# Grouped-query attention on one core: K of two pairs in one buffer, on alternating partitions

## The chip, the cores and the metric

The kernel runs on one core of one Trainium2 chip. The metric is the time of one execution on the device, in microseconds (us). A core has five engines with programs of their own, which meet at semaphores: TensorE (PE), VectorE (DVE), ScalarE (ACT), GpSimd (POOL) and SyncE (SP). Sixteen DMA engines move data between HBM and the on-chip memory SBUF, which has 128 partitions. SP issues nearly all loads here, in the order of its program.

## The reference

```python
B, Hq, Hkv, Sq, Sk, D = 16, 32, 8, 16, 2048, 128      # bf16
k = jnp.repeat(k, 4, axis=1)                           # four query heads share a key head
v = jnp.repeat(v, 4, axis=1)
scores = jnp.einsum("bhqd,bhkd->bhqk", q, k) * D ** -0.5
p = softmax(scores, axis=-1)
return jnp.einsum("bhqk,bhkd->bhqd", p, v)
```

There are 16 x 8 = 128 key heads. Each has 2048 keys and values of 128 numbers (512 KB of K, 512 KB of V) and 4 x 16 = 64 query rows. K and V are 134 MB together, and each byte of them is read once.

## The kernel before

The unit of work is a pair p of neighbouring key heads, 0 to 63: 1 MB of K, 1 MB of V and 128 query rows. Per pair:

- SP loads K into one of eight buffers `Kn` (128 partitions of 8 KB) and V into one of four buffers `Vb`. The helper `load` (L178, issuing through L173) describes a transfer by 64 rows of 16 KB in HBM and 128 rows of 8 KB in SBUF; the first two K loads are plain ones (L285) with 8 KB on both sides.
- DVE turns K with one 32x32-block transpose over 2048 columns of 4 bytes, each holding two bf16 numbers, into one of two buffers `KT` (`kt`, L482; it signals `sem_kt`).
- PE multiplies queries and keys, 32 matmuls into PSUM (`scores`, L353); there is one score buffer `S_ps`, so scores of the next pair wait for `sem_max`.
- DVE evicts and scales the scores in two halves and takes the smallest value of each row (L502; signals `sem_max`). POOL exchanges the row values between the halves of a pair (`exchange`, L225 to L240).
- ACT takes the exponential (L550), PE transposes the result P in eight pieces (L371), ACT evicts them to `PT` (L561), PE multiplies with V (`product`, L423; from pair 56 on in another arrangement, L412), and ACT divides by the row sum (`norm`, L574) and stores.

PE works on `scores(p+1)`, `product(p-4)` and `transposes(p)` in step p. DVE in step p evicts the scores of p, then turns K of p+2.

SP's order of loads is written out by a loop:

```python
for t in range(NP + VLAG):          # NP = 64, VLAG = 6
    if t < NP:
        load_k(t)
    ...                             # Q of four pairs, now and then
    if 0 <= t - VLAG < NP:
        load_v(t - VLAG)
```

SP waits in this order, so a wait holds everything behind it. K of pair p waits until K of pair p-8 has been turned; V of pair p waits until the product of pair p-4 has ended. V of the last four pairs goes into K buffers that are free by then, and waits for `sem_kt`. From pair 56 on (`P4`), V is loaded in two halves, with rows of 8 KB in HBM and 4 KB in SBUF, and the very last V in rows of 3 KB and 1 KB. Outputs go out through `NO` = 8 buffers from ACT's queue up to pair 39; later ones are held in SBUF and stored at the end. In the last steps PE's program is written out by hand, with idle matmuls between products (`IDLE`, L433).

Of the kernel before, what the change touches and what calls it, by code (L numbers as in the profile page):

```python
# [6 lines left out]
ALU = mybir.AluOpType  # L7
# [5 lines left out]
NV = 4  # L13
NKT = 2
NPT = 4
NO = 8
NQ = 2
NR = 8
VLAG = 6
PVLAG = 4  # L20
QLEAD = 3
HELD = (4, 4, 4, 4, 4, 3)
# [3 lines left out]
def bass_standalone__gqa_softmax__sampling_kernel(  # L26
# [3 lines left out]
    v: bass.AP,  # L30
    out: bass.AP,
):

# [21 lines left out]
    sb = lambda name, shape, dt: ctx.enter_context(nc.sbuf_tensor(name, shape, dt))  # L55
    sem = lambda name: ctx.enter_context(nc.semaphore(name))

    iota_t = sb("iota_t", [128, 128], I32)
    ident4 = sb("ident4", [128, 128], F32)
    warm = sb("warm", [128, 2], F32)  # L60
    Kn = [sb(f"Kn{i}", [128, 32 * 128], BF16) for i in range(NK)]
    Vb = [sb(f"Vb{i}", [128, 32 * 128], BF16) for i in range(NV)]
    KT = [sb(f"KT{i}", [128, 32 * 64], F32) for i in range(NKT)]
    Qn = [sb(f"Qn{i}", [128, 4, 128], BF16) for i in range(NQ)]
    Q4 = sb("Q4", [128, 4, 2, 4, 64], BF16)
    QT = [sb(f"QT{i}", [128, 2, 512], F32) for i in range(2)]
# [15 lines left out]
    O_ps = ctx.enter_context(nc.psum_tensor("O_ps", [128, 512], F32))  # L82

    sem_id = sem("sem_id")
    sem_k = [sem(f"sem_k{i}") for i in range(NK)]
    sem_v = [sem(f"sem_v{i}") for i in range(NV)]
    sem_vl = [sem(f"sem_vl{i}") for i in range(2)]
    sem_vx = [sem(f"sem_vx{i}") for i in range(3)]
# [20 lines left out]

    qf = q.rearrange("b h s d -> (b h s) d")  # L110
    of = out.rearrange("b h s d -> (b h s) d")
    kf = k.rearrange("b h s d -> (b h s d)").rearrange("(r x) -> r x", x=4096)
    vf = v.rearrange("b h s d -> (b h s d)").rearrange("(r x) -> r x", x=4096)
    vf4 = v.rearrange("b h s d -> (b h) (s d)").rearrange("g (a x) -> a g x", a=128)

# [15 lines left out]


    def v_tile(p):
        return Kn[p % 4 + (NP - 8) % NK] if p >= NP - 4 else Vb[p % NV]

    def out_tile(p, i):
        return Oh[:, p - PH, :] if isinstance(p, int) and PH <= p < NP - 1 else Osb[i % NO][:, :]
# [48 lines left out]
    with nc.Block() as block:  # L186

        @block.gpsimd
        def _(gp):
            gp.memset(warm[:, :], 0.0).then_inc(sem_id, 1)  # L190
            gp.iota(iota_t[:, :], [[1, 128]], base=0, channel_multiplier=-1).then_inc(sem_id, 1)
            gp.wait_ge(sem_id, 2)
            gp.tensor_scalar(ident4[:, :], iota_t[:, :], 0.0, None, op0=ALU.is_equal).then_inc(sem_id, 1)


            def held(p):
# [79 lines left out]

        @block.sync
        def _(sp):
            def load_k(p):
                s = p % NK  # L280
                if p >= NK:
                    sp.wait_ge(sem_kt, p - NK + 1)
                src = kf[128 * p:128 * (p + 1), :]
                if p < 2:
                    ins = sp.dma_start(Kn[s][:, :], src)  # L285
                else:
                    ins = load(sp, Kn[s][:, :], src, 4096, 2)
                ins.then_inc(sem_k[s], 16)

            def load_v(p):  # L290
                if p >= NP - 4:
                    sp.wait_ge(sem_kt, p - 3)
                elif p >= NV:
                    sp.wait_ge(sem_pv, p - NV + 1)
                dst = v_tile(p)[:, :]
# [12 lines left out]

            def store_held(p, n):
                sp.wait_ge(sem_nm, p + n + 1)  # L310
                src = Oh[:, p - PH:p - PH + n, :]
                copy(
                    sp, of[128 * p:128 * p + 128, :], [[128, 128], [128 * 128, n], [1, 128]],
                    src, [src.ap[0], [1, 1], [1, n * 128]],
                ).then_inc(sem_oh, 16)

            for t in range(NP + VLAG):
                if t < NP:
                    load_k(t)
# [12 lines left out]

        @block.tensor
        def _(pe):
# [3 lines left out]

            def scores(p, i, first=False):
                pe.wait_ge(sem_qs, p + 1)  # L340
                pe.wait_ge(sem_kt, p + 1)
                if not first:
                    pe.wait_ge(sem_max, p)
                kt = KT[i % NKT][:, :].bitcast(BF16).rearrange(
                    "p (w x b l f) -> p w b f x l", w=2, x=16, b=2, l=32)
                qs = Qs[i % 2][:, :, :].rearrange("p b (x f) -> p b f x", f=2)
                for acc in range(4):
                    b, f = divmod(acc, 2)
                    for r in range(4):
                        rows = slice(32 * r, 32 * (r + 1))  # L350
                        h = r // 2
                        for w in range(2):
                            ins = pe.matmul(  # L353
                                S_ps[64 * w:64 * (w + 1), 512 * r:512 * (r + 1)],
                                qs[rows, b, f, 64 * h:64 * (h + 1)],
                                kt[rows, w, b, f],
                                start=(acc == 0), stop=(acc == 3),
                            )
                ins.then_inc(sem_s, 1)
# [29 lines left out]
            def product(p, i, out, tail=False, last=False):  # L389
# [13 lines left out]
                pe.nop(nofuse=True)  # L403
                if isinstance(p, int) and p >= P4:
                    pt = PT[i % NPT][:, :, :].bitcast(BF16).rearrange("p (h t) (w q e) -> p h w t e q", h=2, w=2, e=2)
                    vt = v_tile(p)[:, :].rearrange("p (h j d) -> p h j d", h=2, d=128)
                    for j in range(16):
                        w, t, e = j // 8, j % 8 // 2, j % 2
                        if last and j in (0, 12):
# [5 lines left out]
                            )  # L415
                else:
                    pt = PT[i % NPT][:, :, :].bitcast(BF16).rearrange("p t (w q e) -> p w t e q", w=2, e=2)
                    vt = v_tile(p if isinstance(p, int) else i)[:, :].rearrange("p (x d) -> p x d", d=128)
# [52 lines left out]

        @block.vector
        def _(dve):
            def kt(p, i):
                src = Kn[i % NK][:, :].bitcast(F32)
                dst = KT[i % NKT][:, :]
                if isinstance(p, int) and p >= P4:

                    src = src.rearrange("p (m x y) -> p m x y", m=2, x=8)
                    dst = dst.rearrange("p (x m y) -> p m x y", m=2, x=8)  # L480
                dve.wait_ge(sem_k[i % NK], 2 * (p - i) + 16 * (i // NK + 1))
                ins = dve.transpose(dst, src)  # L482
                ins.then_inc(sem_kt, 1)

# [5 lines left out]
            def step(p, i):  # L490
                known = isinstance(p, int)
                dve.wait_ge(sem_s, p + 1)
                if i >= 2:
                    dve.wait_ge(sem_exp, p - 1)
                for h in range(2):
                    if not known or p < P4:
                        dst = Sneg[i % 2][:, :].rearrange("p (t h g l e) -> p h g t l e", t=8, h=2, g=2, e=2)[:, h]
                        src = S_ps[:, 1024 * h:1024 * (h + 1)].rearrange("p (g t e l) -> p g t l e", g=2, t=8, e=2)
                    else:
                        dst = Sneg[i % 2][:, :].rearrange("p (h t g l f) -> p h g t l f", h=2, t=4, g=2, f=4)[:, h]  # L500
                        src = S_ps[:, 1024 * h:1024 * (h + 1)].rearrange("p (g t f l) -> p g t l f", g=2, t=4, f=4)
                    ins = dve.tensor_scalar(  # L502
                        dst, src,
                        -scale, None, op0=ALU.mult, op1=ALU.min, accum_out=own[:, i % NR, h:h + 1],
                    )
                ins.then_inc(sem_max, 1)
                if i >= 3 and i % 2:
                    recip(p - 3, i - 3, 2)
                if not known or p + 2 < NP:
                    kt(p + 2, i + 2)  # L510

            dve.wait_ge(sem_q[0], 16)
            spread(dve, 0, 1).then_inc(sem_q4d, 2)
# [7 lines left out]
        def _(act):  # L521
# [44 lines left out]
            def norm(p, i):  # L566
# [1 line left out]
                act.wait_ge(sem_pv, p + 1)  # L568
                act.wait_ge(sem_rec, p + 1)
                if not isinstance(p, int) or p < PH:  # L570
                    act.wait_ge(sem_o[i % NO], 2 * (p - i) + 16 * (i // NO + 1))
                elif p == NP - 1:
                    act.wait_ge(sem_o[i % NO], 16 * (PH // NO + 1))
                act.activation(  # L574
# [66 lines left out]
```

## Time and profile before

| | |
|---|---|
| median of 3 runs | 334.89 us (334.74 to 334.95) |
| profiled execution | 334.85 us, its span 333.5 us |
| busy: PE, DVE, ACT, POOL | 279.2, 294.5, 257.7, 149.4 us |
| DMA | 138.61 MB in 19583 packets, 416 GB/s in the mean |
| K loads | 64, of 1 MB, 20.2 us from issue to landing |
| V loads of 1 MB | 56, 18.2 us from issue to landing |
| transposes of K on DVE | 64, 2308 ns each |
| evictions of scores on DVE | 128 halves, 1206 ns each |

Times in a view count from the start of the span. Busy is the time in which an engine ran instructions. A line of the timeline gives start, duration, engine, line of the kernel, operation, and what was written from what; brackets give the idle time ahead of it and what ended it. A view of waits names the waiting engine and line, what ended the wait, the total in us, how often, and the longest. The chain of waits gives start, duration and what; SPq is SP's queue.

### The profile page before, as it was taken

The page shows a single profiled execution, that of the slowest core. Times are in us where ns is not written, and L with a number is a line of the kernel's source. Part 1 is how long each engine was busy: PE and PEld are TensorE (multiplying, and loading weights), DVE is VectorE, ACT ScalarE, POOL GpSimd, SP SyncE. Part 2 cuts the span into 40 slices and gives each one's busy share as a digit, 9 for nine tenths or more (in the row PEclk, how much of TensorE's full clock was granted, in tenths as well). Part 3 has the DMA queues.
Part 4 walks back from the last instruction along what each step waited for, and adds up shares of the span by engine and source line. Part 5 has one row for each costly group of instructions (what it writes and reads, how often), then busy time and mean ns, then how long its engine had stood idle before and what let it go on. Part 6 is the DMA issues. An engine that isn't in the chain of part 4 may idle for free.

```text
span 333.5 us, 16075 instructions
## 1 busy us (share of the span) xinstructions
PE 279.2 (84%) x6542; PEld 209.4 (63%) x6542; DVE 294.5 (88%) x354; ACT 257.7 (77%) x482; POOL 149.4 (45%) x488
## 2 busy tenths in 40 slices
PE   2585988999998999888897988979879798788877
PEld 1253756767676776666665766757757567666465
DVE  3999988999999999989898898998999999989940
ACT  3277877989898989779688787887788687776873
POOL 4444554364544555354445435354363453542320
DMA  8999999999999999999999999999999999999998
GB/s 314 426 419 422 413 419 415 431 424 422 426 423 425 420 428 420 430 418 426 422 427 420 431 419 425 424 423 425 419 421 424 415 423 421 417 425 414 412 405 293
DMA packets 19583, 138.61 MB, mean 416 GB/s; under 512 B 8432, under 2 KB 9712, under 8 KB 10864
## 3 DMA queue, kind: packets, MB, share of 16 engines
q1 hardware_dynamic: 13520, 136.95, 98.1%
q10 hardware_dynamic: 6048, 1.48, 2.0%
q8 instruction: 8, 0.13, 0.2%
q14 instruction: 7, 0.06, 0.0%
HBM read 136.31 MB, written 2.10 MB: 415 GB/s over the span
## 4 chain that ended last, share of the span: by engine, by line
DMA 57%; PE 16%; DVE 15%; issue 8%; ACT 1%; SPq 1%; POOL 1%; DVEq 0%; POOLq 0%; ACTq 0%
DMA Vb<-in_v_dram 43%; PE O_ps L423 9%; DMA Kn<-in_k_dram 8%; DVE KT L482 8%; DVE Sneg L502 7%; DMA Kn<-in_v_dram 5%; PE ST_ps L371 3%; PE S_ps L353 3%; ACT P L550 1%; SPq L173 1%; PE ST_ps L386 1%; POOL nbias L233 0%; PE ST_ps L412 0%; POOL oth L225 0%; POOL oth L228 0%
## 5 line engine op out<-in xcount | busy, mean ns | idle before, releaser
L482 DVE STREAM_TRANSPOSE KT<-Kn 128x2048 f32<-128x2048 f32 x64 | 147.7, 2308 | 20.1 <-DMA Kn<-in_k_dram 19.9
L550 ACT ACTIVATE P<-Sneg,nbias 128x1024 bf16<-128x1024 f32 x128 | 145.9, 1142 | 15.7 <-POOL nbias L233 14.2
L502 DVE TENSOR_SCALAR_CACHE_REDUCE Sneg<-S_ps 128x1024 f32<-128x1024 f32 x128 | 149.9, 1206 | 4.2 <-PE S_ps L353 4.2
L423 PE MATMUL O_ps<-Vb,PT 64*64 64x128 bf16 x3584 | 111.1, 216 | 30.5 <-issue 27.0
L423 PEld LDWEIGHTS O_ps<-Vb,PT 64*64 64x64 bf16 x3584 | 102.8, 107 | 49.3 <-issue 49.3
L561 ACT ACTIVATE PT<-ST_ps 128x512 f32<-128x512 f32 x126 | 68.5, 594 | 16.5 <-PE ST_ps L371 15.9
L353 PE MATMUL S_ps<-KT,Qs 32*64 32x512 bf16 x2048 | 73.5, 396 | 6.0 <-DVE Sneg L502 3.8
L371 PE MATMUL ST_ps<-ident,P 128*128 128x128 f32 x504 | 70.1, 283 | 8.7 <-ACT P L550 8.5
L225 POOL COPY oth<-own 64x4 f32<-64x4 f32 (+1 forms) x65 | 11.9, 183 | 136.4 <-DVE Sneg L502 134.3
L371 PEld LDWEIGHTS ST_ps<-ident,P 128*128 128x128 f32 x504 | 55.1, 143 | 16.9 <-ACT P L550 10.5
L353 PEld LDWEIGHTS S_ps<-KT,Qs 32*64 32x64 bf16 x2048 | 27.3, 106 | 30.4 <-issue 16.6
L207 POOL COPY Qs<-QT 128x512 bf16<-128x512 bf16 x64 | 39.0, 610 | 12.1 <-POOL rowsum L240 5.6
L233 POOL TENSOR_SCALAR nbias<-own,oth 128x1 f32<-128x1 f32 x128 | 33.9, 280 | 10.6 <-POOL oth L228 9.0
L163 POOL COPY Q<-Qn 128x1024 bf16<-128x1024 bf16 x31 | 32.4, 1044 | 1.4 <-DMA Qn<-in_q_dram 1.4
L574 ACT ACTIVATE O<-O_ps,rrec 128x128 bf16<-128x128 f32 x40 | 14.5, 363 | 18.7 <-PE O_ps L423 18.5
L240 POOL TENSOR_TENSOR rowsum<-own,oth 64x1 f32<-64x1 f32 x128 | 23.8, 186 | 8.2
L386 PE MATMUL ST_ps<-ident,Q 128*128 128x128 f32 x128 | 22.5, 304 | 4.6 <-POOL Q L163 4.6
L386 PEld LDWEIGHTS ST_ps<-ident,Q 128*128 128x128 f32 x128 | 14.7, 150 | 18.5 <-issue 18.5
L550 ACT ACTIVATION_READ_ACCUMULATOR P<-Sneg,nbias 128x1 f32 x128 | 24.2, 189 | 0.0
L536 ACT ACTIVATE QT<-ST_ps 128x512 f32<-128x512 f32 x32 | 18.5, 579 | 3.9 <-PE ST_ps L386 3.8
L574 ACT ACTIVATE Oh<-O_ps,rrec 128x128 bf16<-128x128 f32 x20 | 7.3, 367 | 17.3 <-PE O_ps L423 14.4
L228 POOL COPY oth<-own 64x4 f32<-64x4 f32 (+1 forms) x65 | 11.8, 181 | 7.3
(30 smaller groups left out, 44.6 us busy)
## 6 DMA issues: line engine op xcount, KB each, us to landing
Kn<-in_k_dram SPq DMA_DIRECT2D x64, 1024.0 KB, 20.2
Vb<-in_v_dram SPq DMA_DIRECT2D x56, 1024.0 KB, 18.2
Vb<-in_v_dram SPq DMA_DIRECT2D x8, 512.0 KB, 15.4
Kn<-in_v_dram SPq DMA_DIRECT2D x6, 512.0 KB, 14.5
Qn<-in_q_dram SPq DMA_DIRECT2D x15, 128.0 KB, 19.8
out_dram<-O ACTq DMA_DIRECT2D x41, 32.0 KB, 8.9
Kn<-in_v_dram SPq DMA_DIRECT2D x1, 768.0 KB, 17.7
out_dram<-Oh SPq DMA_DIRECT2D x5, 128.0 KB, 11.8
```

Of the source, the lines that this page charges most:

```text
L163: return eng.tensor_copy(Q4[:, :, b, :, :], src.unsqueeze(2).to_broadcast([128, 4, 4, 64]))
L207: gp.tensor_copy(Qs[i % 2][:, :, :], QT[i // 4 % 2][:, :, 128 * x:128 * (x + 1)].bitcast(BF16)).then_inc(sem_qs, 1)
L233: ins = gp.tensor_scalar(nbias[:, s, h:h + 1], own[:, s, h:h + 1], oth[:, s, h:h + 1], None, op0=ALU.min)
L240: gp.tensor_tensor(rowsum[rows, t:t + 1], own[rows, s, 2 + h:3 + h], oth[rows, s, 2 + h:3 + h], op=ALU.add,).then_inc(sem_sum[h], 1)
L353: ins = pe.matmul(S_ps[64 * w:64 * (w + 1), 512 * r:512 * (r + 1)], qs[rows, b, f, 64 * h:64 * (h + 1)], kt[rows, w, b, f], start=(acc == ...
L371: ins = pe.transpose(dst[:, 128 * t:128 * (t + 1)], P[i % 2][:, 128 * x:128 * (x + 1)], ident4[:, :])
L386: ins = pe.transpose(dst[:, 128 * j:128 * (j + 1)], src[:, j, b, :], ident4[:, :])
L423: ins = pe.matmul(out[rows, :], pt[rows, w, t, e, :], vt[rows, x, :], start=(x == 0), stop=(x == 31),)
L482: ins = dve.transpose(dst, src)
L502: ins = dve.tensor_scalar(dst, src, -scale, None, op0=ALU.mult, op1=ALU.min, accum_out=own[:, i % NR, h:h + 1],)
L550: ins = act.activation(to[:, h], of_s[:, h], ACT.Exp, bias=nbias[:, s, h:h + 1], scale=-1.0, accum_out=own[:, t, 2 + h:3 + h],)
L561: act.activation(PT[i % NPT][:, 4 * h:4 * (h + 1), :].rearrange("p t q -> p (t q)"), p_stage_ap(p, h), ACT.Copy,).then_inc(sem_ev[h], 1)
```

## The change

Two pairs, 2n and 2n+1, share a K buffer: there are four buffers `Kn` of 16 KB per partition instead of eight of 8 KB. Each pair lies on every other partition, the even pair on the even partitions, in rows of 16 KB, 64 keys to a row. So one transpose, over half of the columns of a buffer, turns half of the keys of both pairs, and two of them turn both pairs, into one of two buffers `KT` of twice the size. K of the first two pairs is loaded in four transfers of 8 KB rows, by halves of the keys.

With that, scores of an even pair wait for two transposes; the keys come in runs of 16 in `KT`, and the evictions put them in order. DVE turns K three steps ahead instead of two (two in step 0). V lags K by seven places in SP's loop instead of six. There are four output buffers instead of eight, and the table that the identity is made from lies in `KT[1]`.

```diff
-NO = 8
+NO = 4
-VLAG = 6
+VLAG = 7
...
-    Kn = [sb(f"Kn{i}", [128, 32 * 128], BF16) for i in range(NK)]
+    Kn = [sb(f"Kn{i}", [128, 64 * 128], BF16) for i in range(NK // 2)]
-    KT = [sb(f"KT{i}", [128, 32 * 64], F32) for i in range(NKT)]
+    KT = [sb(f"KT{i}", [128, 64 * 64], F32) for i in range(NKT)]
+    iota_t = KT[1][:, 0:128].bitcast(I32)
...
             def load_k(p):
-                s = p % NK
+                n, a = divmod(p, 2)
                 if p >= NK:
-                    sp.wait_ge(sem_kt, p - NK + 1)
-                src = kf[128 * p:128 * (p + 1), :]
-                if p < 2:
-                    ins = sp.dma_start(Kn[s][:, :], src)
-                else:
-                    ins = load(sp, Kn[s][:, :], src, 4096, 2)
-                ins.then_inc(sem_k[s], 16)
+                    sp.wait_ge(sem_kt, 2 * n - NK + 2)
+                dst = Kn[n % (NK // 2)]
+                step = dst[:, :].ap[0][0]
+                for a, y, done in ((a, 0, sem_k[n % (NK // 2)]),) if n else ((0, 4096 * p, sem_kx[p]), (1, 4096 * p, sem_kx[p])):
+                    size = 8192 if n else 4096
+                    r = 64 * (2 * n + a)
+                    copy(
+                        sp, dst[a:a + 1, y:y + size], [[2 * step, 64], [1, 1], [1, size]],
+                        kf[r:r + 64, y:y + size], [[8192, 64], [1, 1], [1, size]],
+                    ).then_inc(done, 16)
 
             def load_v(p):
                 if p >= NP - 4:
-                    sp.wait_ge(sem_kt, p - 3)
+                    sp.wait_ge(sem_kt, p // 2 * 2 - 2)
...
             def scores(p, i, first=False):
                 pe.wait_ge(sem_qs, p + 1)
-                pe.wait_ge(sem_kt, p + 1)
+                pe.wait_ge(sem_kt, p + 2 - i % 2)
...
-                kt = KT[i % NKT][:, :].bitcast(BF16).rearrange(
-                    "p (w x b l f) -> p w b f x l", w=2, x=16, b=2, l=32)
+                kt = KT[i // 2 % NKT][:, :].bitcast(BF16).rearrange(
+                    "p (w x b l a f) -> p w b a f x l", w=2, x=32, b=2, a=2, l=16)
...
-                                kt[rows, w, b, f],
+                                kt[rows, w, b, i % 2, f],
...
             def kt(p, i):
-                src = Kn[i % NK][:, :].bitcast(F32)
-                dst = KT[i % NKT][:, :]
+                n, m = divmod(i, 2)
+                src = Kn[n % (NK // 2)][:, :].bitcast(F32)[:, 2048 * m:2048 * (m + 1)]
+                dst = KT[n % NKT][:, :]
...
+                if n == 0:
+                    dve.wait_ge(sem_kx[m], 32)
+                elif m == 0:
+                    dve.wait_ge(sem_k[n % (NK // 2)], 4 * (p - i) + 32 * (n // (NK // 2) + (n % (NK // 2) > 0)))
                 ins = dve.transpose(dst, src)
...
-                if not known or p + 2 < NP:
-                    kt(p + 2, i + 2)
+                for n in range(2 if known and p == 0 else 3, 4):
+                    if not known or p + n < NP:
+                        kt(p + n, i + n)
```

More of the change, by code (lines that the diff above doesn't have):

```diff
@@ L56, in bass_standalone__gqa_softmax__sampling_kernel @@
     sem = lambda name: ctx.enter_context(nc.semaphore(name))
-    iota_t = sb("iota_t", [128, 128], I32)
     ident4 = sb("ident4", [128, 128], F32)
     warm = sb("warm", [128, 2], F32)
-    Kn = [sb(f"Kn{i}", [128, 32 * 128], BF16) for i in range(NK)]
+    Kn = [sb(f"Kn{i}", [128, 64 * 128], BF16) for i in range(NK // 2)]
     Vb = [sb(f"Vb{i}", [128, 32 * 128], BF16) for i in range(NV)]
-    KT = [sb(f"KT{i}", [128, 32 * 64], F32) for i in range(NKT)]
+    KT = [sb(f"KT{i}", [128, 64 * 64], F32) for i in range(NKT)]
+    iota_t = KT[1][:, 0:128].bitcast(I32)
     Qn = [sb(f"Qn{i}", [128, 4, 128], BF16) for i in range(NQ)]
@@ L84, in bass_standalone__gqa_softmax__sampling_kernel @@
     sem_id = sem("sem_id")
-    sem_k = [sem(f"sem_k{i}") for i in range(NK)]
+    sem_k = [sem(f"sem_k{i}") for i in range(NK // 2)]
+    sem_kx = [sem(f"sem_kx{i}") for i in range(2)]
     sem_v = [sem(f"sem_v{i}") for i in range(NV)]
@@ L111, in bass_standalone__gqa_softmax__sampling_kernel @@
     of = out.rearrange("b h s d -> (b h s) d")
-    kf = k.rearrange("b h s d -> (b h s d)").rearrange("(r x) -> r x", x=4096)
+    kf = k.rearrange("b h s d -> (b h s d)").rearrange("(r x) -> r x", x=8192)
     vf = v.rearrange("b h s d -> (b h s d)").rearrange("(r x) -> r x", x=4096)
@@ L133, in v_tile @@
     def v_tile(p):
-        return Kn[p % 4 + (NP - 8) % NK] if p >= NP - 4 else Vb[p % NV]
+        if p < NP - 4:
+            return Vb[p % NV][:, :]
+        n = p % 4 + (NP - 8) % NK
+        return Kn[n // 2][:, 4096 * (n % 2):4096 * (n % 2 + 1)]
     def out_tile(p, i):
@@ L190, in _ @@
             gp.memset(warm[:, :], 0.0).then_inc(sem_id, 1)
-            gp.iota(iota_t[:, :], [[1, 128]], base=0, channel_multiplier=-1).then_inc(sem_id, 1)
+            gp.iota(iota_t, [[1, 128]], base=0, channel_multiplier=-1).then_inc(sem_id, 1)
             gp.wait_ge(sem_id, 2)
-            gp.tensor_scalar(ident4[:, :], iota_t[:, :], 0.0, None, op0=ALU.is_equal).then_inc(sem_id, 1)
+            gp.tensor_scalar(ident4[:, :], iota_t, 0.0, None, op0=ALU.is_equal).then_inc(sem_id, 1)
             def held(p):
@@ L279, in load_k @@
             def load_k(p):
-                s = p % NK
+                n, a = divmod(p, 2)
                 if p >= NK:
-                    sp.wait_ge(sem_kt, p - NK + 1)
-                src = kf[128 * p:128 * (p + 1), :]
-                if p < 2:
-                    ins = sp.dma_start(Kn[s][:, :], src)
-                else:
-                    ins = load(sp, Kn[s][:, :], src, 4096, 2)
-                ins.then_inc(sem_k[s], 16)
+                    sp.wait_ge(sem_kt, 2 * n - NK + 2)
[8 more added lines that the diff above has]
+                    ).then_inc(done, 16)
             def load_v(p):
                 if p >= NP - 4:
-                    sp.wait_ge(sem_kt, p - 3)
+                    sp.wait_ge(sem_kt, p // 2 * 2 - 2)
                 elif p >= NV:
                     sp.wait_ge(sem_pv, p - NV + 1)
-                dst = v_tile(p)[:, :]
+                dst = v_tile(p)
                 done = sem_vx[p - NP + 4] if NP - 4 <= p < NP - 1 else sem_v[p % NV]
@@ L405, in product @@
                     pt = PT[i % NPT][:, :, :].bitcast(BF16).rearrange("p (h t) (w q e) -> p h w t e q", h=2, w=2, e=2)
-                    vt = v_tile(p)[:, :].rearrange("p (h j d) -> p h j d", h=2, d=128)
+                    vt = v_tile(p).rearrange("p (h j d) -> p h j d", h=2, d=128)
                     for j in range(16):
@@ L417, in product @@
                     pt = PT[i % NPT][:, :, :].bitcast(BF16).rearrange("p t (w q e) -> p w t e q", w=2, e=2)
-                    vt = v_tile(p if isinstance(p, int) else i)[:, :].rearrange("p (x d) -> p x d", d=128)
+                    vt = v_tile(p if isinstance(p, int) else i).rearrange("p (x d) -> p x d", d=128)
                     for x in range(32):
@@ L474, in kt @@
             def kt(p, i):
-                src = Kn[i % NK][:, :].bitcast(F32)
-                dst = KT[i % NKT][:, :]
+                n, m = divmod(i, 2)
+                src = Kn[n % (NK // 2)][:, :].bitcast(F32)[:, 2048 * m:2048 * (m + 1)]
+                dst = KT[n % NKT][:, :]
                 if isinstance(p, int) and p >= P4:
-                    src = src.rearrange("p (m x y) -> p m x y", m=2, x=8)
-                    dst = dst.rearrange("p (x m y) -> p m x y", m=2, x=8)
-                dve.wait_ge(sem_k[i % NK], 2 * (p - i) + 16 * (i // NK + 1))
+                    src = src.rearrange("p (n x y) -> p n x y", n=2, x=8)
+                    dst = dst.rearrange("p (x m n y) -> p m n x y", m=2, n=2, x=8)[:, m]
+                else:
+                    src = src.rearrange("p (x y) -> p x y", x=16)
+                    dst = dst.rearrange("p (x m y) -> p m x y", m=2, x=16)[:, m]
+                if n == 0:
+                    dve.wait_ge(sem_kx[m], 32)
+                elif m == 0:
+                    dve.wait_ge(sem_k[n % (NK // 2)], 4 * (p - i) + 32 * (n // (NK // 2) + (n % (NK // 2) > 0)))
                 ins = dve.transpose(dst, src)
@@ L496, in step @@
                     if not known or p < P4:
-                        dst = Sneg[i % 2][:, :].rearrange("p (t h g l e) -> p h g t l e", t=8, h=2, g=2, e=2)[:, h]
-                        src = S_ps[:, 1024 * h:1024 * (h + 1)].rearrange("p (g t e l) -> p g t l e", g=2, t=8, e=2)
-                    else:
-                        dst = Sneg[i % 2][:, :].rearrange("p (h t g l f) -> p h g t l f", h=2, t=4, g=2, f=4)[:, h]
-                        src = S_ps[:, 1024 * h:1024 * (h + 1)].rearrange("p (g t f l) -> p g t l f", g=2, t=4, f=4)
+                        dst = Sneg[i % 2][:, :].rearrange("p (t h g l f) -> p h g t l f", t=8, h=2, g=2, f=4)[:, h]
+                        src = S_ps[:, 1024 * h:1024 * (h + 1)].rearrange("p (g t f l) -> p g t l f", g=2, t=8, f=4)
+                    else:
+                        dst = Sneg[i % 2][:, :].rearrange("p (h t g l f) -> p h g t l f", h=2, t=4, g=2, f=8)[:, h]
+                        src = S_ps[:, 1024 * h:1024 * (h + 1)].rearrange("p (g t f l) -> p g t l f", g=2, t=4, f=8)
                     ins = dve.tensor_scalar(
@@ L570, in norm @@
                 if not isinstance(p, int) or p < PH:
-                    act.wait_ge(sem_o[i % NO], 2 * (p - i) + 16 * (i // NO + 1))
+                    act.wait_ge(sem_o[i % NO], 16 // NO * (p - i) + 16 * (i // NO + 1))
                 elif p == NP - 1:
```

## The prediction

> **What bounds the kernel now.** I read the page's slices and queues first. GB/s is what the 16 DMA engines moved in each fortieth of the span.
>
> ```profile
> DMA  8999999999999999999999999999999999999998
> GB/s 314 426 419 422 413 419 415 431 424 422 426 423 425 420 428 420 430 418 426 422 427 420 431 419 425 424 423 425 419 421 424 415 423 421 417 425 414 412 405 293
> ...
> q1 hardware_dynamic: 13520, 136.95, 98.1%
> ```
>
> Every inner slice is full and the rate hardly leaves 420. Asked for stretches, the trace gives DMA a share of 1.01 of the 16 engines at 20 to 60, at 100 to 140 and at 240 to 280 us. The bytes set the time; what a compute engine gains or loses in the middle is free while loads stay queued. How deep that queue is, the waits of SP and the chain that ended last tell:
>
> ```profile
> SPq L173 <- PE O_ps L423: 219.2, 56, 18.2
> ```
>
> ```profile
> 287.76 20.38 DMA Kn<-in_k_dram
> 308.16 2.32 DVE KT L482
> ...
> 312.71 17.71 DMA Kn<-in_v_dram
> ...
> 330.46 1.11 PE ST_ps L412 x32
> ...
> 331.60 0.37 ACT O L574
> ```
>
> SP spends 219 us waiting until a product frees a V buffer, and a load issued then lands 18 us later: there are 18 us of queued loads, so a product that is a few us late starves nothing. The last V lands at 330.46, and one product, one division and one store end the kernel. The third view is the timeline of the last 20 us, where compute must be done before that V:
>
> ```profile
> 310.40 1.19 DVE L502 TENSOR_SCALAR_CACHE_REDUCE Sneg<-S_ps 128x1024 f32<-128x1024 f32 x1
> 313.21 2.31 DVE L482 STREAM_TRANSPOSE KT<-Kn 128x2048 f32<-128x2048 f32 x1 [0.39 <-DMA Kn<-in_k_dram]
> 315.44 1.19 DVE L502 TENSOR_SCALAR_CACHE_REDUCE Sneg<-S_ps 128x1024 f32<-128x1024 f32 x1
> 319.11 1.22 DVE L502 TENSOR_SCALAR_CACHE_REDUCE Sneg<-S_ps 128x1024 f32<-128x1024 f32 x1 [1.33 <-PE S_ps L353]
> ```
>
> ```profile
> 322.70 1.15 ACT L550 ACTIVATE P<-Sneg,nbias 128x1024 bf16<-128x1024 f32 x1 [0.17 <-POOL nbias L233]
> ```
>
> ```profile
> 325.13 1.09 PE L371 MATMUL S_ps<-ident,P 128*128 128x128 f32 x8 [0.56 <-ACT P L550]
> 326.15 1.08 PE L412 MATMUL S_ps<-Kn,PT 128*64 128x128 bf16 x32
> 327.17 1.25 PE L433 MATMUL ST_ps<-ident 128*128 128x512 bf16 x5
> 328.57 1.09 PE L412 MATMUL O_ps<-Kn,PT 128*64 128x128 bf16 x32 [0.15 <-issue]
> 329.59 0.82 PE L433 MATMUL ST_ps<-ident 128*128 128x512 bf16 x3
> 330.46 1.10 PE L412 MATMUL ST_ps<-Kn,PT 128*64 128x128 bf16 x32
> ```
>
> The K of pair 63 lands at 313.2, VectorE turns it, evicts the scores of 62 (315.44) and 63 (319.11), ScalarE takes exp 63 at 322.70, TensorE transposes at 325.13, and products 61, 62 and 63 follow with idle matmuls between. That chain is ready for product 63 at 330.41, just as the last V lands: compute has no slack here. Anything that lengthens the way from the last K to product 63 by more than the last V is delayed is added to the end.
>
> **Part 1: the K rows.** 62 of 64 K loads still read 64 rows of 16 KB, but write one row of 16 KB each instead of two of 8 KB. Bytes and source descriptors stay. I take durations from the trace's records of single DMA packets. A 16 KB packet written as two rows takes 618 ns in the mean (7552 of them; hardly one under 611, 614 typical from 60 to 230 us, 625 after). No packet of before writes a row of 16 KB; packets that write one row each are the 3 KB ones of the last V, 125 ns (the fastest tenth 121), and the 8 KB ones of the first two K loads, 309. Drawn on to 16 KB the line through them gives 309 + 8192 x (309 - 125) / 5120 = 603, or 610 with 121. So a packet saves between 611 - 610 = 1 ns and 618 - 603 = 15 ns, times 62 x 64 / 16 = 248 packets per engine: 0.2 to 3.7 us. I take 5 ns, 1.2 us, near the lower end, because the 170 us in the middle run at 614 already. That a packet gets slower is the third rival.
>
> [...]
>
> **Part 2: the order of loads.** VLAG 7 puts K of pair t before V of pair t-7, so V56 stands behind K63 instead of ahead of it. V56 is 128 packets of 8 KB, 128 x 322 / 16 = 2.57 us: K63 lands at 313.2 - 2.57 = 310.6, the last V where it was. A K load now waits for one transpose more when its pair is even (`2 * n - NK + 2`); VectorE turns one pair earlier, so that is free, and SP's wait for products stays the longer one. Behind that wait stand the next K and V, with 18 us of queued loads as cover.
>
> **Part 3: two pairs at once.** One transpose takes half of the keys of both pairs, so `kt(62)` needs K63, and scores of an even pair need both transposes. VectorE's program shows the transpose two pairs early become three early. The count and shape of transposes stay (64 of 2048 columns); the form with 128-column pieces exists already in the last eight, which take 2.31 us like the others. The evictions' new inner order is likewise free: L502 takes 1.18 to 1.22 a half in both orders that exist. In mid-kernel VectorE works 4.5 us a pair (transposes start at 75.31, 79.79 and 84.36) against some 5.1 of DMA, so two pairs in 9.0 fit between two landings of K pairs 10.2 apart. At the start, scores of pair 0 wait for the second transpose, 8.69 instead of 6.21; loads without any product reach to K11 instead of K10 there, 2.5 us more, so it hides.
>
> At the end it does not hide. Behind K63's landing VectorE had one transpose and two evictions; now it has `kt(62)`, Sneg 60, `kt(63)`, Sneg 61, 62 and 63. From start to start: a transpose 2.23 (313.21 to 315.44), an eviction followed at once 2.26, and where no transpose covers the scores matmul a gap of 1.41 (317.70 to 319.11). To the start of Sneg 63: 2.23 + 2.26 + 2.23 + 2.26 + 1.41 + 2.30 + 1.41 = 14.1, where it was 319.11 - 313.21 = 5.9. From 310.6 that gives 324.7 against 319.11, 5.6 later. Behind it everything is as before: exp 3.59 after, product 63 another 7.76 after, all V landed by then. So product 63 starts near 336.1 instead of 330.46. ScalarE and TensorE may absorb a little by working earlier on pairs 60 and 61, or add idle matmuls; I keep 4.7 to 5.9.
>
> **Part 4: the rest.** Four output buffers instead of eight: a store lands in 8.9 us and a buffer comes round after four pairs, 20 us. The iota in KT[1] is read by 2 us, and KT[1] is written after 13 us. Four first K issues of 512 KB instead of two of 1 MB cost SP two issues of some 0.6 us, under 5 us of queued transfer.
>
> **Sum.** The profiled execution took 334.85, 0.04 below the median of the runs. 334.85 + 5.6 - 1.2 = 339.25, and on the median 339.3. Ends of the known terms: + 4.7 - 3.7 = 335.9, + 5.9 - 0.2 = 340.6.
>
> **Rivals.** First, on the other side: the K rows pay more than the tail costs, faster. It decides where a K packet saves over 5.6 / 0.248 = 23 ns (19 ns with the tail at 4.7). For it: late packets are at 625, and the line through the one-row packets has 603 for 16 KB, 22 less. Against: that takes all 248 packets to be late ones, and from 60 to 230 us only 11 are to be had. With 22 ns, 5.5 us, and a tail of 4.7: 334.9 - 5.5 + 4.7 = 334.1. Chance 0.12.
>
> Second, no change within what can be told: a gain at the upper bound, 3.7 us, and a tail of as much because K63 lands 1 us before 310.6, 334.9. Chance 0.04.
>
> Third, writing to every other partition is slower. 64 rows on 16 engines could make two engines share a way into SBUF; the trace before shows no load of 64 rows. [...] If packets of K doubled, 62 x 2.47 = 153 us more, 488; a collision of a tenth, 15 us more, 354. Chance 0.06. [...]
>
> Fourth, TensorE or VectorE becomes the bound: keys are now read in runs of 16 instead of 32. If the 1.10 us of scores doubled, TensorE's 4.4 a pair would be 5.5 against 5.1, some 24 us more, 359. Chance 0.04.
>
> **Numbers.** The forecast has 0.74: 339.3, in itself 335.9 to 340.6. The range leaves the costly rivals out above and the first out below, and adds some tenths for the durations: 335.6 to 341.4. A measurement of this kernel can tell about 0.2%, 0.7 us. Faster 0.12, within it 0.04, slower 0.84.
>
> **What would show it.** Right: slices full until the last V at about 329 to 330; K packets 5 ns shorter; a transpose ended by K near 309 to 311 with two transposes and four evictions behind it; exp 63 near 327; product 63 after the end of the idle matmuls, no longer released by the V load; the end 5 us behind the last V. Wrong: K packets near 600 or above 630, a last V that moved by more than 3 us, DVE or PE without idle time in mid-kernel, or exp 63 before 325.

## The result and the profile after

The changed kernel takes 352.48 us in the median of six runs (351.90 to 353.08), against 334.85 for the kernel before on the same chip. The ratio is 1.052, 95% interval 1.0497 to 1.0543: slower by 17.6 us. The forecast of 339.3 had the sign and a quarter of the size (4.4 of 17.6 us), and 352.48 lies above its range. The profiled execution took 352.15 us, its span 350.8.

The lines of the page after that answer to those shown of before, and the group of the scores matmuls (busy us, mean ns of one, idle time ahead of the group and what ended it):

```profile
PE 327.2 (93%) x6542; PEld 214.5 (61%) x6542; DVE 297.1 (85%) x354; ACT 259.8 (74%) x482; POOL 150.2 (43%) x488
...
GB/s 262 432 430 416 417 386 406 403 372 411 430 425 422 415 428 426 428 418 427 424 421 428 423 426 426 421 425 427 426 418 430 424 418 418 409 347 244 279 379 36
...
q1 hardware_dynamic: 13552, 136.95, 94.5%
...
PE 85%; DVE 7%; issue 3%; DMA 2%; ACT 1%; SPq 1%; POOL 0%; DVEq 0%; ACTq 0%; POOLq 0%
...
L501 DVE STREAM_TRANSPOSE KT<-Kn 128x2048 f32<-128x2048 f32 x64 | 147.1, 2299 | 4.0 <-DMA Kn<-in_k_dram 4.0
L364 PE MATMUL S_ps<-KT,Qs 32*64 32x512 bf16 x2048 | 125.3, 605 | 11.1 <-DVE KT L501 5.8
...
Kn<-in_k_dram SPq DMA_DIRECT2D x62, 1024.0 KB, 9.4
```

TensorE is busy for 327.2 us where it was 279.2, with as many instructions. One group grew: the scores matmuls, 605 ns in the mean, where the page of before has this for the same 2048 matmuls of the same shape:

```profile
L353 PE MATMUL S_ps<-KT,Qs 32*64 32x512 bf16 x2048 | 73.5, 396 | 6.0 <-DVE Sneg L502 3.8
```

The chain that ended last is 85% TensorE and 2% DMA. A K load lands 9.4 us after its issue instead of 20.2: the queue that was 18 us deep has shrunk. Near the end the rate falls to 347, 244 and 279 GB/s: the last K is issued at 304.7 us, only V is left behind it, and SP waits 27.5 us for products between 295 and 332 us. Over the whole span SP's wait for products is 230.7 us, where it was 219.2. The second view is a stretch of the chain in mid-kernel, the third a stretch of 40 us with the busy times in it (PE, PEld, DVE, ACT, POOL, then the granted clock, DMA's share and GB/s):

```profile
SPq L179 <- PE O_ps L434: 230.7, 56, 19.7
```

```profile
185.11 1.91 PE O_ps L434 x64
187.02 1.02 PE ST_ps L382 x8
188.04 1.88 PE S_ps L364 x30
189.93 0.59 PE ST_ps L397 x4
190.51 1.91 PE O_ps L434 x64
192.42 1.02 PE ST_ps L382 x8
193.45 1.88 PE S_ps L364 x30
195.33 1.91 PE O_ps L434 x64
```

```profile
100.00:140.00 40.00, 40.00 (x828) 26.51 (x829) 36.20 (x43) 32.13 (x59) 18.56 (x60) 1.00 1.01 422
```

A step of TensorE is product 1.91, transposes 1.02 and scores 1.88, and in about every other step 0.59 for queries: 5.40 from 185.11 to 190.51, 4.82 to 195.33, 5.1 in the mean. That is what DMA needs for a pair (138.61 MB / 64 at 422 GB/s), and from 100 to 140 us TensorE is busy without a gap. It starts behind: its first product begins at 40.62 us. In the kernel before it began late too, at 33.86, but there the scores of pairs 10 to 50 follow each other every 4.86 us, so compute catches up with the loads; here they follow every 5.11 us. TensorE at 5.11 us a pair, only as fast as the loads, doesn't make up such a start, so its whole program from there on is the time: the last product begins at 347.75.

```profile
347.75 1.09 PE L423 MATMUL ST_ps<-Kn,PT 128*64 128x128 bf16 x32
```

### The profile page after: what moved, and what is told of

It is laid out like the page before. It is cut to its first block, busy times and chain, and to the rows that moved or that the text cites. A ratio compares the mean times of both kernels' runs of the same rounds, so it can differ in the third digit from the quotient of the medians.

```text
span 350.8 us, 16076 instructions
## 1 busy us (share of the span) xinstructions
PE 327.2 (93%) x6542; PEld 214.5 (61%) x6542; DVE 297.1 (85%) x354; ACT 259.8 (74%) x482; POOL 150.2 (43%) x488
## 2 busy tenths in 40 slices
DMA packets 19615, 138.61 MB, mean 395 GB/s; under 512 B 8464, under 2 KB 9744, under 8 KB 10896
## 4 chain that ended last, share of the span: by engine, by line
PE 85%; DVE 7%; issue 3%; DMA 2%; ACT 1%; SPq 1%; POOL 0%; DVEq 0%; ACTq 0%; POOLq 0%
PE S_ps L364 32%; PE O_ps L434 31%; PE ST_ps L382 16%; PE ST_ps L397 5%; DVE KT L501 4%; DVE Sneg L521 3%; DMA Kn<-in_k_dram 2%; ACT P L570 1%; PE ST_ps L444 1%; SPq L179 1%; PE S_ps L382 0%; ACT PT L581 0%; PE ST_ps L423 0%; PE O_ps L423 0%; PE S_ps L423 0%
## 5 line engine op out<-in xcount | busy, mean ns | idle before, releaser
L521 DVE TENSOR_SCALAR_CACHE_REDUCE Sneg<-S_ps 128x1024 f32<-128x1024 f32 x128 | 151.6, 1222 | 35.1 <-PE S_ps L364 33.8
L364 PE MATMUL S_ps<-KT,Qs 32*64 32x512 bf16 x2048 | 125.3, 605 | 11.1 <-DVE KT L501 5.8
L581 ACT ACTIVATE PT<-ST_ps 128x512 f32<-128x512 f32 x126 | 68.3, 594 | 13.8 <-PE ST_ps L382 12.5
L382 PE MATMUL ST_ps<-ident,P 128*128 128x128 f32 x504 | 69.1, 280 | 4.0 <-ACT P L570 4.0
L364 PEld LDWEIGHTS S_ps<-KT,Qs 32*64 32x64 bf16 x2048 | 33.9, 114 | 56.0 <-issue 55.6
L382 PEld LDWEIGHTS ST_ps<-ident,P 128*128 128x128 f32 x504 | 54.2, 142 | 12.9 <-ACT P L570 6.8
```

The costliest lines, as they stand in the source:

```text
L364: ins = pe.matmul(S_ps[64 * w:64 * (w + 1), 512 * r:512 * (r + 1)], qs[rows, b, f, 64 * h:64 * (h + 1)], kt[rows, w, b, i % 2, f], start=( ...
L382: ins = pe.transpose(dst[:, 128 * t:128 * (t + 1)], P[i % 2][:, 128 * x:128 * (x + 1)], ident4[:, :])
L521: ins = dve.tensor_scalar(dst, src, -scale, None, op0=ALU.mult, op1=ALU.min, accum_out=own[:, i % NR, h:h + 1],)
L581: act.activation(PT[i % NPT][:, 4 * h:4 * (h + 1), :].rearrange("p t q -> p (t q)"), p_stage_ap(p, h), ACT.Copy,).then_inc(sem_ev[h], 1)
```

## The experiments

What could make the matmuls slow? In the kernel before, scores reads one bf16 number of each 4-byte column of `KT`, so successive keys are 4 bytes apart. After the change the pairs alternate in `KT` (`l a f`, a the pair), so successive keys of one pair are 8 bytes apart, in runs of 16 instead of 32. Theory A is the step of 8 bytes; theory B is the length of the runs, which is what the prediction's fourth rival named.

### The step back to 4 bytes, with the runs of 16

```diff
-    "p (w x b l a f) -> p w b a f x l", w=2, x=32, b=2, a=2, l=16)
+    "p (w x b a l f) -> p w b a f x l", w=2, x=32, b=2, a=2, l=16)
```

This is the changed kernel but for that line. The runs it reads hold keys of both pairs, so its scores are not those of the reference.

> The changed kernel, but scores reads KT in runs of 16 numbers at a step of 4 bytes instead of 8 bytes (it reads the wrong keys; everything else is kept). Theory A, the 8-byte step slows the matmuls: the 32 matmuls of scores take about 1.05 us a pair again instead of 1.88, TensorE idles in mid-kernel, DMA is the bound and the time is what the prediction had for the tail alone, 339 us (336 to 341). Theory B, the runs of 16 slow them: scores stay at 1.88 us and the time at 352. Theory C, TensorE is not the cause and K's landing is: 352 with scores at 1.05.

Measured: 341.65 us (340.83 to 342.21), ratio to before 1.0177 (1.0120 to 1.0234), just above the 336 to 341 of theory A.

```profile
DMA 36%; PE 20%; DVE 18%; issue 16%; ACT 4%; POOL 3%; SPq 2%; DVEq 0%; POOLq 0%; ACTq 0%
...
L501 DVE STREAM_TRANSPOSE KT<-Kn 128x2048 f32<-128x2048 f32 x64 | 147.5, 2306 | 24.4 <-DMA Kn<-in_k_dram 24.4
...
L364 PE MATMUL S_ps<-KT,Qs 32*64 32x512 bf16 x2048 | 75.9, 403 | 24.7 <-DVE Sneg L521 18.1
```

The matmuls are back at 403 ns, against 396 with runs of 32: the mechanism is theory A's, and B is worth 7 ns at most. DMA leads the chain again, and transposes wait 24.4 us for K. The step costs 352.48 - 341.65 = 10.8 us of the 17.6. The rest, 6.8 us, stays and belongs to something else (below); by the prediction's own terms for tail and rows it would have been 4.4.

### The step of 8 bytes alone, in the kernel before

```diff
-    "p (w x b l f) -> p w b f x l", w=2, x=16, b=2, l=32)
+    "p (w x l b f) -> p w b f x l", w=2, x=16, b=2, l=32)
```

Nothing of the change is in it. The keys that a matmul takes together are others than the reference's.

> The kernel before with one thing of the change alone: scores reads KT at a step of 8 bytes, in runs of 32 (wrong keys). Theory A: scores take 1.88 us a pair, TensorE's work is 1.88 + 1.92 + 1.02 + 0.30 = 5.1 us a pair, equal to DMA's 5.1, so compute never makes up the start (product 0 at 39 us, some 18 us behind the loads) and the time is 350 us (347 to 353). Theory C, the tail of paired K and not TensorE makes the loss: no change from 335.

Measured: 348.70 us (347.79 to 349.69), ratio 1.0381 (1.0324 to 1.0438).

```profile
PE 330.4 (95%) x6542; PEld 210.0 (60%) x6542; DVE 297.0 (85%) x354; ACT 259.7 (75%) x482; POOL 149.4 (43%) x488
...
PE 86%; DVE 7%; issue 3%; DMA 2%; ACT 1%; POOL 0%; SPq 0%; DVEq 0%; ACTq 0%; POOLq 0%
...
L353 PE MATMUL S_ps<-KT,Qs 32*64 32x512 bf16 x2048 | 130.0, 626 | 5.8 <-DVE Sneg L502 3.3
```

One step in one access pattern turns a kernel bound by DMA into one bound by TensorE, 13.8 us slower (334.95 for the kernel before on that chip), without any of the new layout. The runs are no shorter than before, so their length has no part in it. One thing was not as expected: the first product begins at 34.38 us, not at 39. So the loss doesn't need a start much later than the 33.86 of the kernel before; scores follow every 5.19 us, and that is enough.

### Longer runs at a wider step

```diff
-    "p (w x b l a f) -> p w b a f x l", w=2, x=32, b=2, a=2, l=16)
+    "p (w x l a b f) -> p w b a f x l", w=2, x=16, b=2, a=2, l=32)
```

> The changed kernel, but scores reads KT in runs of 32 numbers at the step of 8 bytes (wrong keys). Theory A, the step: scores stay at 1.88 us a pair and the time near 352. Theory B, the runs: 1.05 us and near 339.

The pattern as written steps by 16 bytes, not by the 8 that the expectation speaks of: b moved inside as well. So it doesn't tell what it was meant to tell, but gives a third point. It took 468.13 us, in one run:

```profile
L364 PE MATMUL S_ps<-KT,Qs 32*64 32x512 bf16 x2048 | 245.5, 1077 | 14.0 <-DVE Sneg L521 8.6
```

At steps of 4, 8 and 16 bytes a matmul of 512 columns took 403, 605 and 1077 ns, and the runs of 32 did not help the last. Why a wider step costs more isn't shown.

### Rows of 8 KB on top of the step of 4 bytes

What is left at 341.65 holds the gain by longer rows. In this run K from pair 2 on is written as two rows of 8 KB over all partitions:

```diff
+    if n:
+        copy(sp, dst[:, 4096 * a:4096 * (a + 1)], [[step, 128], [1, 1], [1, 4096]],
+             kf[r:r + 64, :], [[8192, 64], [1, 1], [1, 8192]]).then_inc(done, 16)
+        continue
```

> The kernel of the first run here, but K of pairs 2 to 63 is written as two rows of 8 KB per 16 KB read, over all 128 partitions, as before the change (keys in wrong places; order, waits and bytes kept). The difference to the first run is the worth of 16 KB rows. By the prediction's step 1: 0.2 to 3.7 us slower than the first run, 1.2 at best guess. If rows of 16 KB are worth nothing: the same within 0.7 us. If every other partition costs: faster than the first run.

Measured: 342.65 us (341.61 to 343.29), 1.0 us above the run with long rows; the two sets of runs overlap, so this is a size, not a proof. Three stretches of mid-kernel, first with rows of 16 KB, then of 8 KB (the last column is GB/s):

```profile
100.00:140.00 40.00, 36.27 (x880) 27.75 (x886) 37.00 (x48) 32.98 (x64) 19.13 (x63) 1.00 1.02 427
240.00:280.00 40.00, 34.82 (x848) 26.89 (x848) 36.29 (x45) 31.79 (x62) 18.68 (x60) 1.00 1.01 425
285.00:310.00 25.00, 21.22 (x528) 16.24 (x526) 23.27 (x30) 19.55 (x38) 11.18 (x37) 1.00 1.01 426
```

```profile
100.00:140.00 40.00, 35.29 (x866) 26.73 (x851) 36.05 (x45) 31.83 (x61) 18.96 (x62) 1.00 1.02 425
240.00:280.00 40.00, 34.66 (x848) 26.58 (x848) 36.07 (x45) 31.53 (x61) 18.58 (x60) 1.00 1.01 421
285.00:310.00 25.00, 21.28 (x527) 16.24 (x525) 23.07 (x30) 19.30 (x37) 11.12 (x37) 1.00 1.01 422
```

The long rows bring 427 against 425, 425 against 421 and 426 against 422 GB/s. In the packet records the 16 KB packets (K and V together, 7552 of them) have a median of 611 ns against 616, though their means are 618 and 620. The rate alone, 2 to 4 of 425 over some 250 us, would be worth 1.2 to 2.4 us; 1.0 came out. The run with rows of 8 KB was less short of loads at the start (410 against 383 GB/s from 40 to 70 us), which the rows need not have caused. So rows of 16 KB on every other partition cost nothing on balance and pay about what was forecast; row length and spread change together here, and the run doesn't part them. Nor do the records show the second row of a packet as what costs: from 100 to 140 us 997 of 1008 packets take 611 ns in the run with long rows, V's among them, which are still written as two rows.

### The end and the start, pair by pair

Where do the other 6.8 us lie? The timeline of VectorE at the end of the run with the step of 4 bytes:

```profile
312.20 2.31 DVE L501 STREAM_TRANSPOSE KT<-Kn 128x2048 f32<-128x2048 f32 x1 [1.25 <-DMA Kn<-in_k_dram]
...
316.70 2.31 DVE L501 STREAM_TRANSPOSE KT<-Kn 128x2048 f32<-128x2048 f32 x1
...
322.59 1.23 DVE L521 TENSOR_SCALAR_CACHE_REDUCE Sneg<-S_ps 128x1024 f32<-128x1024 f32 x1 [1.25 <-PE S_ps L364]
...
326.32 1.23 DVE L521 TENSOR_SCALAR_CACHE_REDUCE Sneg<-S_ps 128x1024 f32<-128x1024 f32 x1 [1.35 <-PE S_ps L364]
```

From `kt(62)`, which the last K released, to Sneg 63: 14.12 us. Two runs take the sharing of buffers away at the ends only. First the last eight pairs (`alone`) are loaded, turned and read as in the kernel before, in the halves of the shared buffers; in the second run the first four too, with the order of the first transposes as before. In the middle both keep the step of 4 bytes, over keys of both pairs.

```diff
+    def alone(p):
+        return isinstance(p, int) and p >= 56              # second run: p < 4 or p >= 56
...
+    if alone(p):                                           # load_k
+        load(sp, dst[:, 4096 * a:4096 * (a + 1)], kf[64 * p:64 * (p + 1), :], 4096, 2).then_inc(sem_ku[p], 16)
+        return
...
+    if alone(p):                                           # kt
+        dve.wait_ge(sem_ku[p], 16)
+        dve.transpose(dst[:, 2048 * m:2048 * (m + 1)], src).then_inc(sem_kt, 1)
+        return
```

> The run with runs of 16 keys at a step of 4 bytes (every other partition, one load a pair, keys of the wrong pair among them), and the last eight pairs loaded, turned and read each by itself as in the kernel before. Theory (the two pairs at once cost the end two steps of VectorE): behind the landing of K63 one transpose and three Sneg steps instead of two and four, 14.1 - 2.3 - 2.4 = 9.4 us to Sneg63, so 341.65 - 4.7 = 337.0 us (336.0 to 338.3). Rival (the end is set by the order of the loads or by TensorE's queue): 340.2 or more.

> As the last, and the first four pairs by themselves too, with VectorE's first transposes in the order of the kernel before. Theory (the start costs 3 us because the first two pairs wait for each other's rows, the end 4.7, the rows of 16 KB bring 1 us in the middle): first product near 34 us, 341.65 - 3.1 - 4.7 = 333.9 us (332.8 to 335.2). Rival (the shortage of loads at 44 to 68 us has another cause, such as the granted clock, which was 0.74 at 50 to 55 us): 336 to 338.

Measured: 337.42 us (335.70 to 338.06), ratio 1.0060 (1.0035 to 1.0085), with the last pairs alone; 334.43 us (334.24 to 335.44), ratio 0.9994 (0.9978 to 1.0009), with both ends alone. VectorE from `kt(63)` to Sneg 63, in the first and in the second of them:

```profile
313.03 2.31 DVE L512 STREAM_TRANSPOSE KT<-Kn 128x2048 f32<-128x2048 f32 x1
...
322.64 1.22 DVE L550 TENSOR_SCALAR_CACHE_REDUCE Sneg<-S_ps 128x1024 f32<-128x1024 f32 x1 [1.33 <-PE S_ps L380]
```

```profile
309.34 2.31 DVE L512 STREAM_TRANSPOSE KT<-Kn 128x2048 f32<-128x2048 f32 x1
...
318.92 1.23 DVE L550 TENSOR_SCALAR_CACHE_REDUCE Sneg<-S_ps 128x1024 f32<-128x1024 f32 x1 [1.31 <-PE S_ps L380]
```

9.6 us in both, where the theory had 9.4. In the first run K63 lands at 313.01 us, as VectorE has ended an eviction: load and VectorE are ready within 0.2 us of each other. In the second it lands at 308.94, VectorE comes straight from an eviction, and the landing no longer starts this chain. The last pairs alone save 341.65 - 337.42 = 4.2 us (4.7 expected), the first ones 337.42 - 334.43 = 3.0 (3.1 expected); the runs of one kernel spread over 1.2 to 2.4 us. The start shows where TensorE's scores of pair 0 begin, first with the shared start, then with the first four pairs alone:

```profile
12.65 1.93 PE L380 MATMUL S_ps<-KT,Qs 32*64 32x512 bf16 x32 [6.21 <-DVE KT L524]
```

```profile
8.58 1.93 PE L380 MATMUL S_ps<-KT,Qs 32*64 32x512 bf16 x32 [2.22 <-DVE KT L512]
```

Between 40 and 70 us the loads run at 393 GB/s in the one and at 422 in the other. The second run had the lower granted clock at the start (0.87 in the first 40 us against 1.00), so the clock is not what slows the start. But the first product begins at 37.24 us in the second run (40.06 in the first), not near 34 as expected; that pairs 4 and 5 are turned together ahead of it may be why.

So all 17.6 us have a place: step 10.8, end 4.2, start 3.0, less about 0.4 that the kernel with both ends alone lies under the kernel before, which is within its interval. The sizes hold for this order of taking the parts away: by itself, in the kernel before, the step costs 13.8. The gain of 1 us by the rows of 16 KB, which the expectation counted on, can't be told from that.

### Can the pairs be kept apart elsewhere?

Two places are left to separate the pairs, so that scores reads the right keys at 4 bytes: VectorE's writing, and the placing by the loads. First VectorE:

```diff
-    dst = dst.rearrange("p (x m y) -> p m x y", m=2, x=16)[:, m]
+    dst = dst.rearrange("p (x m u a l) -> p m x u l a", m=2, x=16, u=4, a=2)[:, m]
```

> The changed kernel, with the two pairs kept apart where VectorE writes the turned keys: each transpose writes runs of 16 words at a time, first those of one pair of heads and then, 64 bytes on, those of the other, so that scores reads runs of 16 keys at a step of 4 bytes, as in the run with that step (341.65), and here the keys are the right ones. The last eight pairs are turned by two half transposes each. Theory A (the step at which TensorE reads is the whole loss; where VectorE writes costs nothing): scores 403 ns, transposes stay at 2306 ns each, 341.6 us (340.8 to 342.5). Rival D (a write in pieces costs VectorE): VectorE has about 4.6 us of work a pair of heads against the loads' 5.1, so up to some 0.4 us on a transpose stays hidden; a transpose of 4.6 us would make VectorE the bound at 7 us a pair, some 460 us; of 3.0 us, some 350 us.

Measured: 402.05 us (401.70 to 403.89), ratio 1.2027 (1.1994 to 1.2060).

```profile
PE 290.0 (72%) x6542; PEld 215.9 (54%) x6542; DVE 377.5 (94%) x362; ACT 255.3 (64%) x482; POOL 149.4 (37%) x488
...
DVE 61%; issue 33%; PE 3%; DMA 1%; DVEq 1%; ACT 0%; SPq 0%; POOL 0%; ACTq 0%; POOLq 0%
...
L505 DVE STREAM_TRANSPOSE KT<-Kn 128x2048 f32<-128x2048 f32 x56 | 214.2, 3830 | 4.0 <-DMA Kn<-in_k_dram 4.0
L364 PE MATMUL S_ps<-KT,Qs 32*64 32x512 bf16 x2048 | 77.6, 411 | 74.7 <-DVE Sneg L525 66.5
```

The scores are quick, 411 ns, and the transpose takes 3830 ns instead of 2306: rival D. (As written, its output alternates between the two runs word by word, 64 bytes to and fro; whole runs at a time, as the expectation puts it, would be another pattern, and weren't tried.) The 1.5 us more per pair passes VectorE's slack and VectorE becomes the bound, busy 94% of the span. (The evictions took longer as well, 1336 ns instead of 1205; why isn't shown.)

Then the loads: pair 0 on partitions 0 to 15, 32 to 47 and so on, in four loads of 16 rows.

```diff
-    copy(sp, dst[a:a + 1, y:y + size], [[2 * step, 64], [1, 1], [1, size]],
-         kf[r:r + 64, y:y + size], [[8192, 64], [1, 1], [1, size]]).then_inc(done, 16)
+    for g in range(4):
+        r, z = 64 * (2 * n + a) + 16 * g, 32 * g + 16 * a
+        copy(sp, dst[z:z + 1, y:y + size], [[step, 16], [1, 1], [1, size]],
+             kf[r:r + 16, y:y + size], [[8192, 16], [1, 1], [1, size]]).then_inc(done, 16)
```

> The changed kernel with the pairs on blocks of 16 partitions instead of every other one: pair 0 on partitions 0 to 15, 32 to 47 and so on, pair 1 on those between. VectorE's transpose is that of the changed kernel, and behind it the keys of a pair stand in runs of 16 at a step of 4 bytes, as scores read them in the run with that step, and here the keys are the right ones. [...] Theory A (the step at which TensorE reads, set by where the rows are laid): scores 403 ns, transposes 2306 ns, 341.6 us (340.8 to 342.5). Rival E (loads of 256 KB have a price): 192 more loads on the queue; at 20 ns each 345.5, at 50 ns 351.

> The kernel with blocks of 16, and the last eight pairs loaded, turned and read each by itself as in the kernel before (rows of 8 KB over all partitions, in the buffer's halves), with the order of VectorE's steps left as changed. Theory (the two pairs at once cost the end two steps): behind the landing of K63 stand one transpose and three Sneg steps instead of two transposes and four, so 14.1 - 2.3 - 2.4 = 9.4 us to Sneg63, and 4.7 us less than the kernel with blocks alone, 337.0 where that gives 341.65. Rival (the end is set by the loads' order or by TensorE's queue behind it): within 1.5 us of the kernel with blocks.

> As the last, and the first four pairs by themselves too, with VectorE's first transposes in the order of the kernel before. Theory (the start costs 3 us because pairs 0 and 1 wait for each other's rows; the end 4.7; the rows of 16 KB bring 1 us in the middle): the first product back near 34 us, and 341.65 - 3.1 - 4.7 = 333.9 us (332.8 to 335.2), about 1 us under the kernel before. Rival (the dip of the loads at 44 to 68 us has another cause, such as the granted clock): the start stays, 337.

Measured: 724.08 us (719.60 to 732.59) with all pairs in blocks, 674.15 (651.69 to 698.49) with the last eight pairs alone, 634.40 (620.15 to 653.83) with both ends alone. Neither theory had this, and the last two runs say nothing of the ends, as the loads in blocks bound them. With all pairs in blocks, transposes keep their 2308 ns but wait 417.1 us for K, and the loads have lost more than half of their rate:

```profile
GB/s 140 118 122 127 189 169 169 157 193 168 198 203 190 210 208 200 203 200 193 189 197 186 194 185 188 196 187 202 201 192 197 199 196 201 212 204 200 195 346 160
...
Kn<-in_k_dram SPq DMA_DIRECT2D x248, 256.0 KB, 35.7
```

Is it the size of a load or the neighbouring partitions? Two more runs keep the 16 KB rows and change the spread: four loads of 16 rows on every eighth partition, and two of 32 rows on every fourth. Both read scores as in the run with the step of 4 bytes, keys of both pairs together.

```diff
-        r, z = 64 * (2 * n + a) + 16 * g, 32 * g + 16 * a
-        ... [[step, 16], ...          ... [[8192, 16], ...
+        r, z = 64 * (2 * n + a) + g, 2 * g + a
+        ... [[8 * step, 16], ...      ... [[4 * 8192, 16], ...     # second: range(2), 4 * step, 2 * 8192, 32 rows
```

> The run with runs of 16 keys at a step of 4 bytes, and K of a pair in four loads of 16 rows of 16 KB as in the kernel with blocks, but each load on every eighth partition instead of on 16 partitions side by side. Theory S (loads of 256 KB, 16 rows, are slow in themselves): as the kernel with blocks, near 724 us, 190 GB/s. Theory N (16 partitions side by side are what is slow): near the run with one load, 342 to 350 us, 426 GB/s. Between the two: the rate goes by how widely a load spreads over the partitions. [...]

> As the run with loads of 16 rows on every eighth partition, but K of a pair in two loads of 32 rows of 16 KB, each on every fourth partition, over all 128 partitions. Three layouts are known: one load of 64 rows on every other partition, 341.65 us; four of 16 on every eighth, 561; four of 16 side by side, 724. Theory S (the smaller a load, the slower, whatever it reaches): between the first two, 400 to 500 us. [...]

Measured: 560.98 us with loads of 16 rows spread (two runs at 548.40 and 550.07, two at 571.89 and 573.43), 342.74 (342.15 to 344.18) with loads of 32 rows, where theory S had 400 to 500. Slices of the first and of the second:

```profile
GB/s 194 226 222 277 244 258 269 261 250 250 226 246 251 259 271 271 259 268 270 250 272 272 256 280 270 275 263 267 260 236 249 246 257 265 259 259 259 216 382 70
```

```profile
GB/s 249 417 413 426 428 359 384 389 376 425 427 425 426 421 426 427 423 432 422 429 426 426 425 428 419 428 426 427 425 422 419 428 425 425 422 422 412 410 370 62
```

Loads of the same 256 KB gave 190 or 253 GB/s in the mean of the page, by where they put their rows, so size is not all of it; twice as many loads as in the changed kernel, of 512 KB and well spread, gave 404 in the mean and 425 in most slices. By what way the spread counts is not shown. What a load of 16 rows costs by itself, spread over everything, was not tried, and between 16 and 32 rows a load both its size and its spread change.

## Why the prediction was wrong, and where it was right

- **The step that failed** is the sentence of Part 3 that VectorE works 4.5 us a pair against 5.1 of DMA, so that all fits in mid-kernel, with the one before Part 1 that what a compute engine loses in the middle is free while loads stay queued. Part 3 looked at VectorE alone; TensorE's scores were left in the sum at their 1.10 us a pair, a change put at nothing without a reason. Their read pattern changed: `l a f` for `l f`, 8 bytes for 4. A matmul went from 396 to 605 ns, scores from 1.10 to 1.95 us a pair in the timeline, and TensorE's busy time from 279.2 / 64 = 4.4 to 327.2 / 64 = 5.1 us a pair, as much as DMA's. This missing term is worth 10.8 us.
- **The fourth rival** had the engine, but a wrong reason: runs of 16 instead of 32, which cost 7 ns at most. That its 359 lies near 352.48 is in part luck: it has 24 us for TensorE, where 10.8 were found (13.8 by itself), and nothing for start and end, which make up the rest. Argued from the run length it got 0.04. The diff showed the step; with it on paper, the slack of 0.7 us a pair would have been the number to compare.
- **The start does not hide.** The first transpose starts at 7.51 us instead of 6.21, since pairs 0 and 1 land by halves, and the first scores at 12.47 instead of 8.66: 3.8 us later, where Part 3 had the 2.5 from 6.21 to 8.69. Later steps of the start, in which VectorE turns two pairs between evictions, add to it: the first product starts at 40.62 (40.12 with the step of 4 bytes) instead of 33.86. The 2.5 us of further loads that were to cover it do not cover more than 6, and in the run with the step of 4 bytes the rate falls to 351 GB/s in one slice near 55 us. Measured 3.0 us (first pairs alone or not), forecast 0.
- **The end was sized rightly.** With the step at 4 bytes 14.12 us pass from the last K's transpose to Sneg 63, forecast 14.1; product 63 starts 25.13 us after it (337.33), forecast 14.1 + 3.59 + 7.76 = 25.45. The last eight pairs alone save 4.2 us, less than the 5.6: that run keeps VectorE's changed order, so 9.6 us are left from the transpose to Sneg 63, where the kernel before had 5.9. In the changed kernel itself this chain stands behind TensorE's queue: K63 lands at 314.11 us, and `kt(62)` starts at 320.30.
- **The K rows:** 5 ns a packet and 1.2 us forecast; 5 ns in the median packet and 1.0 us measured, with overlapping runs. The size came out, the reason didn't: V's packets of two rows got as short as K's (from 100 to 140 us 997 of 1008, both together, took 611 ns).
- **K63's landing** was to come at 310.6; in the run with the step of 4 bytes it came at 312.2, and with the first four pairs alone at 308.9. That points to the lost start.
- **The first three rivals fall:** the rows never came near 23 ns a packet, nor did their gain reach 3.7 us, and every other partition gave 425 to 427 GB/s. That the rate can depend on the partitions a load writes, as the third has it, the runs with 16 rows a load show (190 GB/s in the mean with the rows side by side, 253 on every eighth partition); whether engines share a way into SBUF there, they don't.
- **Evictions and transposes** kept their times, 1205 and 2306 ns in the run with the step of 4 bytes. Of the signs named for a wrong forecast two came in the changed kernel: TensorE without idle time in mid-kernel, 40.00 us busy in 40 from 100 to 140 us, and a last V that moved by more than 3 us, from about 330.4 to about 341.8.

## What to carry to other kernels

Where a layout changes, write out the step in bytes of every operand that reads it, on TensorE too, before calling an instruction unchanged because its count and shape are. Then compare each engine's time per round with the bound's time per round: an engine equal to it was already too slow here, as it didn't make up for a late start (scores every 5.11 and 5.19 us against 5.1 of loads). And ask where an interleave is paid that is free for the loads, as every other partition was here (425 to 427 GB/s): in the three places tried it was by the reader's step (605 ns a matmul for 403), by the writer's (3830 ns a transpose for 2306), or by the partitions that a load writes (190 GB/s in the mean for 407).

## What the hardware showed that was not expected

- A scores matmul (512 columns, 32 rows) took 403, 605 and 1077 ns with its moving operand at steps of 4, 8 and 16 bytes.
- A 32x32-block transpose of 128x2048 took 2306 ns when written in order, and 3830 ns when its output alternated between places 64 bytes apart.
- With V loads between them, K loads of 16 KB rows left a rate of 190, 253 and 404 GB/s in the mean (425 in most slices of the last) with 16 rows side by side, 16 rows on every eighth partition, and 32 rows on every fourth.
- The granted clock was 0.99 in the changed kernel (TensorE busy 93%) and 0.83 and 0.76 in the kernels with loads of 16 rows (63% and 54%); with 72%, in the kernel whose transposes write apart, it was still 0.996 in the profiled execution.
